# One matrix's load cut differently: w2 in runs of 14 half rows, the remainder in sixteen one-partition loads of prime length on GpSimd's queue

## The chip, the cores and the metric

The kernel runs on one core of a Trainium2 chip, alone. The metric is the device time of one execution in microseconds, as a median of several runs. One profiled execution goes with it: its trace lists every instruction of the compute engines (PE is TensorE, DVE is VectorE, ACT is ScalarE, POOL is GpSimd, SP is SyncE, which here only issues transfers), every packet that the core's 16 DMA engines moved, and every update of a semaphore. "DMA engine" below always means one of those 16; they are not the compute engines.

## The reference

One token passes through two blocks whose results are added: attention over a cache of 65,536 keys in four groups, and a mixer MLP. What matters here:

```
xn = layernorm(x)                                   # x: 1 x 1024
A: q = xn @ wq;  scores, softmax and values over k_cache, v_cache; @ wo
B: h  = gelu(layernorm(xn) @ w1)                    # w1: 1024 x 1024
   g0 = pad(h[:, :, 0:c], ((0,0),(1,0),(0,0)))[:, :S]      # and three more quarters,
   ...                                                     # shifted along the sequence
   hs = concat([g0, g1, g2, g3]) @ w2               # w2: 1024 x 1024
   x1 = xn + hs
   h2 = gelu(layernorm(x1) @ w3) @ w4               # w3: 1024 x 3584, w4: 3584 x 1024
out = x + A + (x1 + h2)
```

The sequence has one token, S = 1, so each of the four quarters is shifted out of sight and `hs` is zero whatever w2 holds. The kernel still loads all of w2 (2 MB, bfloat16) and multiplies it by a column of zeros, `g_col`. All operands are bfloat16; some 170 MB are read, 134 MB of them the two caches.

## The kernel before, in words

Three buffers of 64 KB per partition, `slot0` to `slot2`, take in turn everything that is loaded: wq, w3, w1 with w2, then for eight units K and V (64 KB on each partition, 8 MB a load), then wo, then w4 in five pieces. The list `stream` sets that order and `freed(it)` issues the load that comes three places later, as soon as the instructions that read the slot are recorded. All these loads are issued by SP, in order, and SP waits at each one until its slot is free.

A class `Program` records every operation, and `plan()` derives the waits: an instruction waits for the writers of what it reads and for the readers and writers of what it overwrites. Every transfer has a semaphore of its own that counts to 16. For POOL alone `plan` also makes each operation wait for the one before it on that engine (`last_pool`). The text of `emit` hands the instructions out in the recorded order.

w1 and w2 share a slot (`w12`). Each partition holds 8 rows of w1 (16 KB). w2 is seen as 2,048 half rows of 512 elements (1 KB). A run of `W2_RUN` = 15 of them goes to each of the 128 partitions, in one transfer. The remaining 128 half rows go by `W2_EXTRAS` in two further transfers, on SP too: 20 half rows on each of the partitions 0, 4, 8, 12, 16, and 14 on each of the partitions 1 and 5. Behind the run every partition has room for `W2_DEEP` = 20 half rows. POOL clears that room first (the memset of 128 x 5,120 words), since most partitions get no extra half rows and the multiplication goes over all partitions. The product with w2 is 15 + 20 = 35 matmuls into `psB` (`row_acc` with `g_col`, in `compute_w12`), after which `freed("w12")` issues K of unit 1.

Where the work stands on the queues around the change: POOL makes the identity, the masks and the memsets, the last of them the room behind w2's run, and then copies the queries into `qdiag` when they are there (`place_queries`). SP issues wq at the start, then w3, then w1, w2's run and the two extras. PE waits for w3, w1 and w2 in that order, and DVE starts the first unit's transposes when K of unit 0 has landed.

At the end the fifth piece of w4 (`W4_PIECES`, the last one row of 2 KB per partition) lands, four narrow matmuls use it, ACT and DVE copy the result out, and ACT stores it.

Of the kernel before, what the change touches and what calls it, by code (L numbers as in the profile page):

```python
# [14 lines left out]
P = 128  # L15
# [7 lines left out]
WIDTH = {F32: 4, BF16: 2}  # L23
PITCH = {}
HALF = 512
W2_RUN = 15
W2_EXTRAS = ((0, 5, 20), (1, 2, 14))


def regions(ap):  # L30
# [15 lines left out]
def meet(a, b):  # L46
    return a[0] == b[0] and a[1] < b[2] and b[1] < a[2] and a[3] < b[4] and b[3] < a[4]
# [11 lines left out]
class Program:  # L59
# [74 lines left out]
    def plan(self):  # L134

        known = {e: {} for e in self.engines}
        count = {e: 0 for e in self.engines}
        writers, readers, last_pool = {}, {}, None
        for n, op in enumerate(self.ops):
            e, op.n = op.engine, n  # L140
            need = {}

            def needs(other, raw):
                if other.queue == e and (e in self.IN_ORDER or not raw):
                    return
                if known[e].get(other.queue, 0) < other.at:
                    if other.queue not in need or need[other.queue].at < other.at:
                        need[other.queue] = other

            for r in op.reads:  # L150
                for region_, other in writers.get(r[0], ()):
                    if meet(r, region_):
                        needs(other, True)
            for w in op.writes:
                for region_, other in writers.get(w[0], ()):
                    if meet(w, region_):
                        needs(other, True)
                for region_, other in readers.get(w[0], ()):
                    if meet(w, region_):
                        needs(other, False)  # L160
            if e == "pool" and last_pool is not None:
                needs(last_pool, True)
            picked = sorted(need.values(), key=lambda o: o.n)
            kept = [o for o in picked
                    if not any(o is not x and x.clock.get(o.queue, 0) >= o.at for x in picked)]
            for o in kept:
                o.awaited = True
                for q, at in o.clock.items():
                    known[e][q] = max(known[e].get(q, 0), at)
            op.waits = kept  # L170
            if op.transfer:
                op.queue, op.at = ("dma", n), 1
            else:
                count[e] += 1
                op.queue, op.at = e, count[e]
            if e == "pool":
                last_pool = op
            op.clock = dict(known[e])
            op.clock[op.queue] = op.at
            for w in op.writes:  # L180
                for table in (writers, readers):
                    kept_ = [(r, o) for r, o in table.get(w[0], ())
                             if not (w[1] <= r[1] and r[2] <= w[2] and w[3] <= r[3] and r[4] <= w[4])]
                    table[w[0]] = kept_
                writers[w[0]].append((w, op))
            for r in op.reads:
                readers.setdefault(r[0], []).append((r, op))
# [29 lines left out]
def kernel(  # L217
# [15 lines left out]
    D = A_x.shape[-1]  # L233
# [17 lines left out]
    prog = Program(nc)  # L251
    pe, dve, act, pool = prog, prog.dve, prog.act, prog.pool

    def sb(name, shape, dtype=F32):
        return nc.alloc_sbuf_tensor(name, list(shape), dtype)
# [3 lines left out]

    slots = [sb(f"slot{i}", [P, ROW], BF16) for i in range(3)]  # L260
    PITCH.update({t[:].tensor.name: ROW * 2 for t in slots})
    W2_DEEP = max(m for _, _, m in W2_EXTRAS)
    assert sum(k * m for _, k, m in W2_EXTRAS) == D * D // HALF - P * W2_RUN
    p_sb = sb("p_sb", [P, SUBS * 512], BF16)
    og = sb("og", [P, 512])
    x_row = sb("x_row", [32, D], BF16)
# [32 lines left out]
    tiles = {it: slots[i % 3] for i, it in enumerate(stream)}  # L299

    def load(it):
        t = tiles[it]
        if it == "wq":
            prog.load("sp", t[:], A_wq.rearrange("(p c) n -> p (c n)", c=DC))
        elif it == "w3":
            prog.load("sp", t[:, 0:DC * F], B_w3.rearrange("(p c) f -> p (c f)", c=DC))
        elif it == "w12":
            prog.load("sp", t[:, 0:DC * D], B_w1.rearrange("(p c) n -> p (c n)", c=DC))
            at = DC * D
            halves = B_w2.rearrange("r (h n) -> (r h) n", n=HALF)  # L310
            first = P * W2_RUN
            prog.load("sp", t[:, at:at + W2_RUN * HALF], halves[0:first, :].rearrange("(m c) n -> m (c n)", c=W2_RUN))
            at += W2_RUN * HALF
            for b, k, m in W2_EXTRAS:
                prog.load("sp", t[b:b + 4 * k - 3:4, at:at + m * HALF],
                          halves[first:first + k * m, :].rearrange("(q c) n -> q (c n)", c=m))
                first += k * m
        elif it == "wo":
            prog.load("sp", t[:], A_wo.rearrange("(p j) n -> p (j n)", p=P))
        elif it == "w4":  # L320
            w4_v = B_w4.rearrange("(m c) n -> m c n", c=FC)
            c0 = 0
            for n in W4_PIECES:
                prog.load("sp", t[:, c0 * D:(c0 + n) * D], w4_v[:, c0:c0 + n, :].rearrange("p c n -> p (c n)"))
                c0 += n
        else:
            kind, i = it
            g, b = divmod(i, NB)
            cache = A_k_cache if kind == "K" else A_v_cache
            prog.load("sp", t[:], cache[0, g, b * UKEYS:(b + 1) * UKEYS, :].rearrange("(p ct) d -> p (ct d)", p=P))  # L330

    def freed(it):

        n = stream.index(it) + 3
        if n < len(stream):
            load(stream[n])

    load("wq")
    opening = len(prog.ops)

    dve.memset(x_row[:], 0.0)
    prog.load("act", x_row[0:1, :], A_x[0, 0:1, :])
    load("w3")

    pool.memset(ident_f[:], 0.0)
# [14 lines left out]
    pool.memset(g_col[:], 0.0)  # L360
    w2_end = DC * D + (W2_RUN + W2_DEEP) * HALF
    pool.memset(tiles["w12"][:, w2_end - W2_DEEP * HALF:w2_end].bitcast(F32), 0.0)
    load("w12")

    def row_acc(j, lhsT, rhs, start=False):
        return pe.mm(psB[32 * j:32 * j + 32, :], lhsT.to_broadcast([P, 32]), rhs, start, False, (0, 32 * j), COLS)
# [7 lines left out]
    def layernorm(src, tag):  # L374
        rowsum = sb(f"ln_rowsum_{tag}", [P, 1])
        dve.reduce_sum(out=rowsum[:], in_=src[:], axis=AX.X)
        at = next_pm()
        pe.mm32(at[:, 0:1], ones_f[:], rowsum[:], True, True)
        negmean = sb(f"ln_negmean_{tag}", [P, 1])
        dve.tensor_scalar(out=negmean[:], in0=at[:, 0:1], scalar1=-1.0 / D, scalar2=None, op0=ALU.mult)  # L380
        cen = sb(f"ln_cen_{tag}", [P, DC])
        dve.tensor_scalar(out=cen[:], in0=src[:], scalar1=negmean[:, 0:1], scalar2=None, op0=ALU.add)
        sq = sb(f"ln_sq_{tag}", [P, DC])
        rowsq = sb(f"ln_rowsq_{tag}", [P, 1])
        dve.tensor_tensor_reduce(out=sq[:], in0=cen[:], in1=cen[:], scale=1.0, scalar=0.0,
                                 op0=ALU.mult, op1=ALU.add, accum_out=rowsq[:])
        pe.mm32(at[:, 1:2], ones_f[:], rowsq[:], True, True)
        std = sb(f"ln_std_{tag}", [P, 1])
        act.activation(out=std[:], in_=at[:, 1:2], func=ACTF.Sqrt, bias=eps_t[:, 0:1], scale=1.0 / D)
        rstd = sb(f"ln_rstd_{tag}", [P, 1])  # L390
        dve.reciprocal(out=rstd[:], in_=std[:])
        normed = sb(f"ln_out_{tag}", [P, DC])
        dve.tensor_scalar(out=normed[:], in0=cen[:], scalar1=rstd[:, 0:1], scalar2=None, op0=ALU.mult)
        rep = sb(f"ln_rep_{tag}", [P, DC, 32], BF16)
        dve.tensor_copy(out=rep[:], in_=normed[:].unsqueeze(2).to_broadcast([P, DC, 32]))
        return normed, rep, negmean, rstd

    xn, xn_rep, negmean1, rstd1 = layernorm(xT, "a")
    _, xn2_rep, _, _ = layernorm(xn, "b")
# [53 lines left out]
    def compute_w12():  # L453
# [6 lines left out]
        act.activation(out=h1, in_=sc[0:32, 0:2, :], func=ACTF.Gelu_apprx_tanh)  # L460
        for c in range(W2_RUN + W2_DEEP):
            row_acc(c % 2, g_col[:], wt[:, 2 * DC + c, :], start=(c < 2))
# [86 lines left out]
    for u in range(NU):  # L549
        g, b = divmod(u, NB)  # L550
# [11 lines left out]
    o = tiles["w4"][0:64, FC * D:FC * D + D].bitcast(F32)  # L562
# [76 lines left out]
```

## Time and profile before

| | |
|---|---|
| time, median of 3 runs | 400.24 us (400.12 to 400.31) |
| time of the profiled execution | 400.13 us |
| its span in the trace | 398.8 us |
| busy: PE, DVE, ACT, POOL | 226.0, 210.2, 27.6, 10.6 us |
| mean granted TensorE clock | 0.795 |
| landings on the sixteen DMA engines of the last piece of w4, from the trace's semaphore updates | 394.94, 394.96, 395.29, 395.64, 395.71, 396.29, 396.33, 396.48, 396.49, 396.52, 396.57, 396.65, 396.68, 396.73, 396.74, 396.79 us |

The span leaves 1.33 us of the execution's time outside of it. In the profile's lists a line begins with the source line and engine; `out<-in` are the program's tiles without their buffer number, so `slot` is any of the three slots, and `in_B_w_dram` any of w1 to w4. L92, L99 and L116 are the lines of the recording helpers, so operations are told apart by tiles. A time in square brackets in a timeline is how long the engine sat idle before, and for whom.

### The profile page before, as it was taken

What the parts mean: (1) busy time and instruction counts of PE and PEld (TensorE: products, weight loads), DVE (VectorE), ACT (ScalarE), POOL (GpSimd) and SP (SyncE); (2) the same over time, 40 slices, a digit from 0 to 9 for tenths busy, and PEclk for the clock granted to TensorE, in tenths of its full rate; (3) what the DMA queues carried; (4) which work ended last, traced back from release to release, by engine and by line L of the source; (5) the groups of instructions that cost most, each with busy time, mean ns of one, the idle gap of its engine ahead of it and who ended that gap; (6) DMA issues with size and microseconds to landing.
All of it is one profiled execution on the core that took longest, in us unless ns stands there. A gap on an engine that the chain in (4) does not pass through costs nothing.

```text
span 398.8 us, 2582 instructions
## 1 busy us (share of the span) xinstructions
PE 226.0 (57%) x1379; PEld 45.2 (11%) x890; DVE 210.2 (53%) x156; ACT 27.6 (7%) x35; POOL 10.6 (3%) x30
## 2 busy tenths in 40 slices
PE   0250990592469256923874197529552946393587
PEld 0210000010101020001001000201010102010233
DVE  0520010975096549653963795259439932793411
ACT  1010030002000200020002000200010011002000
POOL 7000000000000000000000000000000000000000
PEclk9996797597859666978796779568967995687669
DMA  8989999999999999999999999999999999999996
GB/s 342 493 375 419 470 427 421 435 460 434 429 421 434 427 435 434 440 440 434 416 434 440 434 421 442 440 427 427 427 449 440 421 434 435 427 427 421 409 438 274
DMA packets 3774, 170.03 MB, mean 426 GB/s; under 512 B 426, under 2 KB 428, under 8 KB 685
## 3 DMA queue, kind: packets, MB, share of 16 engines
q1 hardware_dynamic: 3758, 169.87, 98.8%
q8 instruction: 9, 0.15, 0.1%
q14 instruction: 1, 0.01, 0.0%
q10 hardware_dynamic: 6, 0.00, 0.0%
HBM read 169.87 MB, written 0.00 MB: 426 GB/s over the span
## 4 chain that ended last, share of the span: by engine, by line
DMA 62%; PE 20%; DVE 15%; ACT 2%; issue 0%; SPq 0%
DMA slot<-in_A_k_cache_dram 44%; DMA slot<-in_B_w_dram 18%; PE sc L116 14%; DVE slot L92 11%; PE oacc L116 4%; DVE p_sb L92 2%; DVE mx L92 2%; ACT p_sb L92 2%; PE psB L116 1%; PE pm L132 0%; DVE m L92 0%; DVE rep L92 0%; DVE nball L92 0%; DVE x_halves L92 0%; PE pm L116 0%
## 5 line engine op out<-in xcount | busy, mean ns | idle before, releaser
L116 PE MATMUL sc<-slot,qdiag 128*128 128x512 bf16 x512 | 130.9, 418 | 65.7 <-DVE slot L92 65.6
L92 DVE STREAM_TRANSPOSE slot<-slot 128x4096 f32<-128x4096 f32 x32 | 139.4, 4411 | 52.2 <-DMA slot<-in_A_k_cache_dram 52.2
L116 PE MATMUL oacc<-slot,p_sb 128*32 128x512 bf16 x512 | 44.5, 524 | 37.5 <-DVE p_sb L92 18.8
L92 DVE STREAM_TRANSPOSE p_sb<-p_sb 128x2048 bf16<-128x2048 bf16 (+2 forms) x10 | 20.8, 2085 | 38.7 <-ACT p_sb L92 38.5
L92 DVE TENSOR_REDUCE mx<-sc 128x1 f32<-128x2048 f32 x8 | 18.3, 2292 | 30.6 <-PE sc L116 30.6
L112 PEld LDWEIGHTS <-qdiag 128*128 128x128 bf16 x128 | 13.2, 103 | 181.4 <-issue 181.4
L92 ACT ACTIVATE p_sb<-sc,nball 128x2048 bf16<-128x2048 f32 x8 | 15.7, 1967 | 250.7 <-DVE nball L92 250.7
L112 PEld LDWEIGHTS <-p_sb 128*32 128x32 bf16 x512 | 16.3, 127 | 62.4 <-issue 19.8
L116 PE MATMUL sc<-slot,ln_rep_b 128*32 128x512 bf16 (+1 forms) x80 | 16.2, 828 | 9.1 <-DMA slot<-in_B_w_dram 8.9
L132 PE MATMUL pm<-ident_f,mx 128*1 128x128 f32 x8 | 2.2, 270 | 19.1 <-DVE mx L92 19.1
L92 DVE SCALAR_TENSOR_TENSOR og<-oacc,wb,og 128x512 f32<-128x512 f32 x4 | 3.0, 751 | 18.8 <-PE oacc L116 18.8
L92 POOL COPY qdiag<-qx 32x32 bf16<-32x32 bf16 x16 | 3.2, 203 | 272.5 <-PE sc L116 250.6
L116 PE MATMUL psB<-slot,oT 128*32 128x512 bf16 x64 | 9.2, 457 | 1.2 <-DVE oT L92 1.2
L126 PE MATMUL pm<-ol,selx 128*128 128x129 f32 x8 | 2.6, 415 | 10.6 <-DVE ol L92 10.6
L116 PE MATMUL sc<-slot,ln_rep_a 128*32 128x512 bf16 x64 | 5.7, 532 | 4.4 <-DMA slot<-in_A_wq_dram 4.4
L126 PE MATMUL pm<-ln_rowsum_a,msk 128*128 128x1 f32 x2 | 0.6, 362 | 13.3 <-DVE ln_rowsum_a L92 13.3
L92 DVE TENSOR_TENSOR og<-psB,slot 64x512 f32<-64x512 f32 x1 | 0.7, 683 | 13.1 <-PE psB L116 13.1
L92 DVE STREAM_TRANSPOSE p_sb<-x_row 32x256 bf16<-32x256 bf16 x4 | 2.5, 616 | 7.4 <-DMA x_row<-in_A_x_dram 7.4
L116 PE MATMUL psB<-slot,g_col 128*32 128x512 bf16 x35 | 4.9, 379 | 0.0
L132 PE MATMUL pm<-ident_f,rep 1*128 1x1 f32 x8 | 1.9, 234 | 5.0 <-DVE rep L92 5.0
L92 ACT COPY og<-oacc 128x512 f32<-128x512 f32 x4 | 2.3, 585 | 32.1 <-PE oacc L116 32.1
L116 PE MATMUL psB<-slot,hT 128*32 128x512 bf16 x40 | 4.5, 379 | 0.0
(87 smaller groups left out, 65.5 us busy)
## 6 DMA issues: line engine op xcount, KB each, us to landing
slot<-in_B_w_dram SPq DMA_DIRECT2D x1, 7168.0 KB, 37.3
slot<-in_B_w_dram SPq DMA_DIRECT2D x2, 2048.0 KB, 37.8
slot<-in_B_w_dram SPq DMA_DIRECT2D x1, 3072.0 KB, 33.4
slot<-in_B_w_dram SPq DMA_DIRECT2D x1, 1920.0 KB, 47.2
slot<-in_B_w_dram SPq DMA_DIRECT2D x1, 1280.0 KB, 33.2
slot<-in_B_w_dram SPq DMA_DIRECT2D x1, 512.0 KB, 34.1
slot<-in_B_w_dram SPq DMA_DIRECT2D x1, 256.0 KB, 34.2
slot<-in_A_k_cache_dram SPq DMA_DIRECT2D x8, 42.2
```

The costliest lines, as they stand in the source:

```text
L92: return program.add(Op(engine, lambda: method(*args, **kw), reads, writes, alone=kw.get("accum_out") is not None))
L112: self.add(Op("pe", lambda: pe.ldweights(lhsT, tile_position=pos), [lhsT], []))
L116: return pe.add_instruction(mybir.InstMatmult(name=nc.get_next_instruction_name(), engine=mybir.EngineType.PE, start_tensor_calc=start, st ...
L126: return self.add(Op("pe", lambda: pe.matmul(out, lhsT=lhsT, rhs=rhs, start=start, stop=stop, tile_position=pos, skip_group_check=True), [ ...
L132: return self.add(Op("pe", lambda: pe.transpose(out, in_, identity), [in_, identity], [out]))
```

## The change

- `W2_RUN` goes from 15 to 14: each partition's run is 14 KB.
- The other 256 half rows, 131,072 elements, are cut into sixteen stretches of consecutive elements, each a prime number of elements long (17,401 down to 1,021), and a remainder of 86 elements. Each goes to one partition: 0, 4, ..., 28 for the first eight, 64, 68, ..., 92 for the other eight, and 32 for the remainder.
- The sixteen are issued by POOL, right behind its memset; the remainder by SP, ahead of w1.
- `W2_DEEP` becomes 34, so the memset covers 128 x 8,704 words, and the multiplication with `g_col` has 14 + 34 = 48 matmuls.
- `plan` no longer makes a POOL operation that is a transfer wait for the one before it, nor the next one for the transfer.

```diff
-W2_RUN = 15
-W2_EXTRAS = ((0, 5, 20), (1, 2, 14))
+W2_RUN = 14
+W2_EXTRAS = (17401, 16889, 10223, 11261, 16381, 1021, 1531, 15859, 2557, 3067, 3583, 4093, 4603, 6653, 7673, 8191)
...
-            if e == "pool" and last_pool is not None:
+            if e == "pool" and last_pool is not None and not op.transfer:
                 needs(last_pool, True)
...
-            if e == "pool":
+            if e == "pool" and not op.transfer:
                 last_pool = op
...
-    W2_DEEP = max(m for _, _, m in W2_EXTRAS)
-    assert sum(k * m for _, k, m in W2_EXTRAS) == D * D // HALF - P * W2_RUN
+    W2_DEEP = -(-max(W2_EXTRAS) // HALF)
+    W2_REST = D * D - P * W2_RUN * HALF - sum(W2_EXTRAS)
+    assert 0 < W2_REST <= W2_DEEP * HALF
...
             prog.load("sp", t[:, at:at + W2_RUN * HALF], halves[0:first, :].rearrange("(m c) n -> m (c n)", c=W2_RUN))
-            at += W2_RUN * HALF
-            for b, k, m in W2_EXTRAS:
-                prog.load("sp", t[b:b + 4 * k - 3:4, at:at + m * HALF],
-                          halves[first:first + k * m, :].rearrange("(q c) n -> q (c n)", c=m))
-                first += k * m
...
     pool.memset(tiles["w12"][:, w2_end - W2_DEEP * HALF:w2_end].bitcast(F32), 0.0)
+    w2_flat = B_w2.rearrange("r n -> (r n)")
+    first = P * W2_RUN * HALF
+
+    def w2_piece(engine, p, n):
+        at = w2_end - W2_DEEP * HALF
+        prog.load(engine, tiles["w12"][p:p + 1, at:at + n], w2_flat[first:first + n].rearrange("(o n) -> o n", o=1))
+
+    for e, n in enumerate(W2_EXTRAS):
+        w2_piece("pool", 64 * (e // 8) + 4 * (e % 8), n)
+        first += n
+    w2_piece("sp", 32, W2_REST)
     load("w12")
```

## The prediction, made before the changed kernel ran

> **What bounds the kernel now.** First the page's head: the span, the strip of DMA activity in 40 slices, the queue table and the chain that ended last.
>
> ```profile
> span 398.8 us, 2582 instructions
> ...
> DMA  8989999999999999999999999999999999999996
> ...
> q1 hardware_dynamic: 3758, 169.87, 98.8%
> q8 instruction: 9, 0.15, 0.1%
> ...
> q10 hardware_dynamic: 6, 0.00, 0.0%
> HBM read 169.87 MB, written 0.00 MB: 426 GB/s over the span
> ...
> DMA 62%; PE 20%; DVE 15%; ACT 2%; issue 0%; SPq 0%
> ```
>
> The strip shows the sixteen DMA engines at nine tenths or more nearly everywhere, while PE and DVE are busy 57% and 53%. The chain also names PE and DVE because it passes through instructions that free a slot; but SP issues each load long before the one ahead of it has drained, so the engines have work all the time. The kernel ends when the slowest of the sixteen has moved its share. The end of the chain, in order of time:
>
> ```profile
> 362.56 34.22 DMA slot<-in_B_w_dram
> 396.79 0.04 issue
> 396.83 0.34 PE pm L116 x4
> 397.19 0.43 DVE x_halves L92
> ```
>
> The last piece of w4 lands at 396.79; the 2.0 us behind it are fixed. So the question is which engine lands last, and when.
>
> For that I followed the trace's packet records. A 64 KB packet takes 2.42 us and the next one on its engine starts where it ends, so sixteen chains separate. The sixteen last landings (394.94 to 396.79, mean 396.18) then have reasons. Two engines carry 34 extra half rows and land at 396.29 and 396.33; of the three that carry 20, two land at 395.64 and 395.71, and one, which also moved an 8 KB code packet, near the end. Of the eleven without extras, three land at 394.94, 394.96 and 395.29, and eight at 396.48 or later. Each of these eight has one of PE's code packets in it (the q8 line: nine of 16 KB), which costs its engine about 1.5 us, a gap of 1.0 to 1.1 and a lengthened 64 KB packet. The nine start at 43.3, 104.2, 145.2, 195.9, 242.1, 297.5, 336.4, 377.5 and 396.65; the ninth comes when the last data packet (ends 396.33) is through.
>
> **The change, part by part.** The bytes are the same; only their place changes. A packet of 20 half rows took 0.761 us, so a half row is worth 0.038 us of its engine.
>
> *Shares.* If each prime load is one unsplit transfer on one engine, in turn, engine e gets 14 x 8 half rows and 34, 33, 20, 22, 32, 2, 3, 31, 5, 6, 7, 8, 9, 13, 15, 16, where before it had 15 x 8 and 34, 34, 20, 20, 20 and none. The differences are -8, -9, -8, -6, +4, -6, -5, **+23**, -3, -2, -1, 0, +1, +5, +7, +8, in time -0.34 to +0.87 us. Perfect levelling would bring 396.79 down to the mean, 396.18: 0.61 us is all that there is to gain. The trace doesn't say which engine number each of the eleven chains has. If engine 7 is one of the eight with a code packet (8 chances in 11), it lands at 396.48 to 396.74 plus 0.87: 0.56 to 0.82 later than now, 0.7 in the middle. If it is one of the three early ones, it lands by 396.2, and the end falls to whichever of engines 13, 14, 15 (+0.19 to +0.30) is late: 0.1 to 0.3, say 0.2. Weighted, 0.73 x 0.7 + 0.27 x 0.2 = 0.56; I take **+0.5 us**.
>
> *Are they unsplit?* The nearest row is the one-row load of x, 2 KB: q10's six packets are that load's and the store's, one data packet and one semaphore packet of the load. A row of one partition stays whole on one engine there. That was ACT's queue; for POOL's nothing is shown (a rival below).
>
> *A second queue beside the stream.* The same load shows how a small queue fares:
>
> ```profile
> 2.98 0.53 ACTq L99 DMA_DIRECT2D x_row<-in_A_x_dram  x1
> ...
> 10.35 2.50 DVE L92 STREAM_TRANSPOSE p_sb<-x_row 32x256 bf16<-32x256 bf16 x4 [7.40 <-DMA x_row<-in_A_x_dram]
> ```
>
> Issued at 2.98, it lands at 10.35: in the records its data packet starts at 7.50 and its semaphore packet at 9.99, one 64 KB packet later. So a second queue gets one packet in turn with the stream. It cost the stream 0.07 us for 2 KB, its own bytes and no more. That is the lower bound, and I take it, as the nearest kind (data into a slot's memory). The upper bound is the code packet: 16 KB cost 1.5 us where its bytes at 0.038 are 0.6, a factor of 2.5. At that factor 31 to 34 half rows cost up to 2.0 us more, on engine 7 on top of +0.7: **+2.7 us**. Semaphore packets took 9 ns each; if every load puts one on every engine, 16 are 0.15 us, and I add nothing, since the stream's own 27 show no gap.
>
> *When they land.* Turn by turn, up to 17 packets an engine from about 14 us on: 3 turns in wq's rest, 8 in w3 (its 56 KB packets, to 39.3), 6 of w1's 16 KB packets: all landed by 45 us, before w2's run at 50.
>
> ```profile
> 5.62 4.36 POOL L92 MEMSET slot<- 128x5120 f32 x1
> 31.20 1.00 POOL L92 COPY qdiag<-qx 32x32 bf16<-32x32 bf16 x4 [21.22 <-DVE qx L92]
> ...
> 2.30 9.25 SPq L99 DMA_DIRECT2D slot<-in_B_w_dram  x5
> ...
> SPq L99 <- POOL slot L92: 6.3, 1, 6.3
> ```
>
> *POOL and SP.* The memset grows by 8,704/5,120, to 7.4 us, and ends at 13.0. SP's wait for it, which now stands ahead of w1 at the 86-element load, grows from 6.3 to 9.4; queued behind it are w1 and w2's run, issued by 14.5, while wq and w3 occupy the engines to 39.6: hidden by 25 us. Sixteen issues on POOL cost between SP's 0.33 and ACT's 0.53 us, doubled for safety 17 us: POOL is free at 30, just when the copies into `qdiag` come at 31.2. Those are needed for the first scores, at 74:
>
> ```profile
> 55.71 4.25 PE L116 MATMUL psB<-slot,g_col 128*32 128x512 bf16 x32
> ...
> 59.99 0.33 SPq L99 DMA_DIRECT2D slot<-in_A_k_cache_dram  x1
> 69.75 8.77 DVE L92 STREAM_TRANSPOSE slot<-slot 128x4096 f32<-128x4096 f32 x2 [15.77 <-DMA slot<-in_A_k_cache_dram]
> 74.25 2.29 PE L116 MATMUL sc<-slot,qdiag 128*128 128x512 bf16 x5 [14.29 <-DVE slot L92]
> ```
>
> *PE.* Thirteen more matmuls at 4.25/32 = 0.13 are 1.7 us, and PE waits for 17 semaphores more or less in a row. PE sits idle for 14.29 us behind them; K of unit 1, issued behind them at 59.99, would go out at 61.7 with K and V of unit 0 (to 89 us) still ahead of it. Nothing. Without that cover it would be the 1.7 us.
>
> *Sum.* Span 398.8 + 0.5 = 399.3, execution 400.13 + 0.5 = 400.6; the median stands 0.11 above the profiled execution, so **400.7 us**.
>
> **Rivals.**
> *Foreign packets dear* (slower). POOL's packets cost the stream as code packets do. For: the code packets are the only large foreign ones. Against: the 2 KB load. One or two tenths of the worst case to all of it: +1.0 to +2.7, about 402.2. It decides once the factor is above about 1.3. The Trainium skill (DMA: Bandwidth & Descriptors, Latency and other measured facts) says engines 7 and 15 are usually slower, with software descriptor rings as its guess at the cause; here all sixteen chains show 2.42 us packets without such a queue, so the trace before can't refute it, and the change puts its +23 on engine 7 and +8 on 15.
> *The ninth code packet moves into the end* (slower). PE gets 13 matmuls and 7 wait instructions more, so the ninth fetch comes 20 instructions earlier. PE was 20 records back at about 395.9, so the fetch would start near 396.0, with late engines still moving data to 396.33. If it falls on one of them, their last landing moves by 0.7 to 1.5: with the shares, 401.3. Against: the first eight fell on eight different engines, and most of those left are early.
> *The numbers fit* (faster). Engine 7 early, 13 to 15 not late: -0.1 to -0.6, about 399.9, never below 399.5.
> *They are not spread.* All sixteen on the first engine: 256 half rows against its 34, less 8 of the run, +214 x 0.038 = 8.1 us on an engine that now lands 0.5 early: +7.6, 407.8. For: x's single row is one packet on a single engine. Splitting a prime row element by element is a worse version: 17,401 packets of 9 ns are 157 us, hidden nowhere. The Trainium skill (same page, Why a DMA increments its semaphore by 16 and not by 1) lets a transfer of undividable length use one engine, the next of a rotating cursor on POOL's path, which is the forecast; it also notes direct copies dealt out as partitions over sixteen, which for one partition is this rival. No row here tells.
>
> **How the numbers follow.** Forecast 0.50; dear packets 0.16; ninth packet 0.13; fitting numbers 0.14; not spread 0.07. Forecast's own range is 400.2 to 401.1. The range must leave out the unspread case and the tails: 399.7 to 402.7. Runs of this kernel differ by 0.1 us, and 0.2%, 0.8 us, is about what a measurement tells from no change: 399.4 and 401.0. Faster than that is out of reach of levelling (0.61): 0.05 for what I don't see. Slower: dear packets 0.15, ninth 0.12, unspread 0.07, the forecast's upper tail 0.09: 0.43. Within: 0.52.
>
> **What would show it.** Right: sixteen prime data packets on sixteen engines between 14 and 45 us, 64 KB packets still 2.42 us, the chain's last landing near 397.3, PE idle still about 12 us before the first scores. Wrong: a chain of DMA engine 7 that isn't late, a code packet before the last landing, gaps in the stream beside POOL's packets longer than their bytes, or one engine with all of them and a last landing past 404.

## The result, and the profile after

The changed kernel takes 414.20 us (median of 4 runs, 413.82 to 414.45) where the kernel before takes 400.18 us beside it: a ratio of 1.0349, 95% interval 1.0331 to 1.0367. The forecast was 400.7 us, the range 399.7 to 402.7.

The head of the page after, as it was shown of the kernel before:

```profile
span 412.5 us, 2616 instructions
...
DMA  9998999999999999999999999999999999998950
...
q1 hardware_dynamic: 3746, 169.61, 95.8%
q0 software_dynamic: 512, 0.26, 0.3%
...
HBM read 169.87 MB, written 0.00 MB: 412 GB/s over the span
...
DMA 42%; DVE 26%; PE 21%; another core or an unknown queue 7%; ACT 3%; issue 1%
```

The bytes are the same, but the strip of DMA activity now ends in 8, 9, 5, 0: for the last slices most engines are done. The end in stretches (length, busy time of PE, PEld, DVE, ACT and POOL, granted clock, share of the sixteen DMA engines, GB/s):

```profile
395.00:397.00 2.00, 1.98 (x10) 0.76 (x12) 0.54 (x1) 0.00 (x0) 0.00 (x0) 0.50 0.94 381
397.00:399.00 2.00, 2.00 (x12) 0.78 (x10) 0.00 (x0) 0.00 (x0) 0.00 (x0) 0.50 0.31 122
399.00:404.00 5.00, 5.00 (x46) 2.20 (x42) 0.00 (x0) 0.00 (x0) 0.00 (x0) 0.92 0.06 25
404.00:409.00 5.00, 5.00 (x62) 2.47 (x60) 0.18 (x1) 0.00 (x0) 0.00 (x0) 1.00 0.08 29
```

From 399 to 409 us the DMA share is 0.06 to 0.08 at 25 to 29 GB/s. One engine of sixteen is 0.0625 and 27 GB/s (64 KB in 2.42 us). So **one engine works alone for the last 12 us**. The sixteen landings of the last piece of w4 say the same: fifteen between 396.82 and 398.50, one at 410.45 (before: 394.94 to 396.79). Every load from K of unit 0 on has one landing 12 to 13 us behind the rest. A unit can start only with its last landing, so PE and DVE run late by as much; the chain shows them and the DMA engines by turns. At the very end it shows PE:

```profile
395.02 13.77 PE psB L116 x104
...
410.20 0.63 PE pm L116 x12
```

PE gets to wo and w4 only then (64 and 40 of these matmuls), with a granted clock of 0.50 until 399 us (the last column but two of the stretches above). Its last four matmuls still start 0.05 us behind the landing at 410.45, so the landing sets the end here too, but PE has no more than about 0.2 us to spare.

The packet records don't number the engines, but a packet starts where the one before it on its engine ends, and so the chain of the late engine can be followed. All sixteen prime loads are whole: sixteen data packets of 34,802 down to 2,042 bytes on POOL's queue, q0, and 496 packets of 4 bytes beside them. But all sixteen data packets stand on the *same* engine, each with two packets of the stream between it and the next for most of the way: at 19.61, 23.33, 29.68, 35.23, 41.08 and so on to 62.75 us. The landings of POOL's loads, by size (KB, us from issue to landing):

```profile
slot<-in_B_w_dram POOLq DMA_DIRECT2D x1, 34.0 KB, 10.4
slot<-in_B_w_dram POOLq DMA_DIRECT2D x1, 33.0 KB, 14.1
...
slot<-in_B_w_dram POOLq DMA_DIRECT2D x1, 15.0 KB, 42.2
slot<-in_B_w_dram POOLq DMA_DIRECT2D x1, 16.0 KB, 43.7
```

They land in the order of issue, the smaller later ones last: one line of waiting, not sixteen.

The places that the prediction costed at nothing, from the timelines and SP's waits:

```profile
5.59 7.35 POOL L92 MEMSET slot<- 128x8704 f32 x1
13.24 8.31 POOL L99 DMA_DIRECT2D slot<-in_B_w_dram  x16 [0.30 <-POOL slot L92]
...
SPq L99 <- POOL slot L92: 10.4, 1, 10.4
...
64.63 5.36 PE L116 MATMUL psB<-slot,g_col 128*32 128x512 bf16 x48
70.02 0.33 SPq L99 DMA_DIRECT2D slot<-in_A_k_cache_dram  x1
83.69 8.77 DVE L92 STREAM_TRANSPOSE slot<-slot 128x4096 f32<-128x4096 f32 x2 [21.13 <-DMA slot<-in_A_k_cache_dram]
88.19 4.43 PE L116 MATMUL sc<-slot,qdiag 128*128 128x512 bf16 x10 [18.20 <-DVE slot L92]
```

POOL's memset and issues are done at 21.6, and PE still idles 18.20 us before the first scores. None of them is on the path; DVE waits for K of unit 0, whose last landing is at 83.67.

So 214 half rows too many on one engine explain 8.1 us there, 7.6 at the end, since that engine used to land 0.5 us before the last one. But the end moved by 410.45 - 396.79 = 13.7. The rest, 6 us, had to be found. The fifteen others are late as well: they land 1.7 to 1.9 us later at either end of their field (396.82 against 394.94, 398.50 against 396.79), though each of them carries at least 8 half rows less than before.

### The profile page after: what moved, and what is told of

It is laid out like the page before. It is cut to its first block, busy times and chain, and to the rows that moved or that the text cites. A ratio compares the mean times of both kernels' runs of the same rounds, so it can differ in the third digit from the quotient of the medians.

```text
span 412.5 us, 2616 instructions
## 1 busy us (share of the span) xinstructions
PE 228.4 (55%) x1392; PEld 46.0 (11%) x890; DVE 210.3 (51%) x156; ACT 27.6 (7%) x35; POOL 21.9 (5%) x46
## 4 chain that ended last, share of the span: by engine, by line
DMA 42%; DVE 26%; PE 21%; another core or an unknown queue 7%; ACT 3%; issue 1%
DMA slot<-in_A_k_cache_dram 31%; DVE slot L92 18%; DMA slot<-in_B_w_dram 11%; PE sc L116 11%; PE oacc L116 6%; PE psB L116 3%; DVE p_sb L92 3%; DVE mx L92 3%; ACT p_sb L92 3%; PE pm L132 1%; DVE og L92 1%; PE pm L126 0%; DVE m L92 0%; DVE rep L92 0%
## 5 line engine op out<-in xcount | busy, mean ns | idle before, releaser
L116 PE MATMUL sc<-slot,qdiag 128*128 128x512 bf16 x512 | 129.1, 412 | 68.6 <-DVE slot L92 68.5
L116 PE MATMUL oacc<-slot,p_sb 128*32 128x512 bf16 x512 | 47.4, 551 | 37.5 <-DVE p_sb L92 18.8
L112 PEld LDWEIGHTS <-p_sb 128*32 128x32 bf16 x512 | 17.4, 132 | 64.3 <-issue 23.3
L99 POOL DMA_DIRECT2D slot<-in_B_w_dram x16 | 8.3, 528 | 0.3 <-POOL slot L92 0.3
L92 POOL MEMSET slot<- 128x8704 f32 x1 | 7.4, 7351 | 0.1
L112 PEld LDWEIGHTS <-ln_rep_b 128*32 128x32 bf16 x40 | 1.9, 112 | 30.4 <-issue 30.3
## 6 DMA issues: line engine op xcount, KB each, us to landing
slot<-in_B_w_dram SPq DMA_DIRECT2D x1, 1792.0 KB, 50.9
```

Source lines behind the costliest of these rows:

```text
L92: return program.add(Op(engine, lambda: method(*args, **kw), reads, writes, alone=kw.get("accum_out") is not None))
L99: return self.add(Op(engine, lambda: e.dma_start(out=out, in_=in_), [], [out], transfer=True))
L112: self.add(Op("pe", lambda: pe.ldweights(lhsT, tile_position=pos), [lhsT], []))
L116: return pe.add_instruction(mybir.InstMatmult(name=nc.get_next_instruction_name(), engine=mybir.EngineType.PE, start_tensor_calc=start, st ...
```

## The experiments

Each kernel is compared with runs of the kernel before on the same chip, 400.2 to 400.3 us throughout.

**Who keeps the loads on one engine: the queue or the shape?** The same loads, issued by SP.

```diff
-        w2_piece("pool", 64 * (e // 8) + 4 * (e % 8), n)
+        w2_piece("sp", 64 * (e // 8) + 4 * (e % 8), n)
```

> The sixteen prime loads are issued by SP instead of POOL, all else as in the changed kernel. Theory 'one row, one engine': a load of one partition stays on one DMA engine, the same one each time, whatever the queue; the bytes alone then put 214 half rows x 0.038 = 8.1 us on it, and the last landing comes 7.6 us later than in the kernel before: 407.8 us, up to 414 if the extra 6 us of the changed kernel come from writing into distant partitions and not from having two queues. Rival 'POOL's queue is at fault': issued by SP the loads spread or cost their bytes on sixteen engines: 400 to 401 us. In both, the fifteen other engines lose their 32 small packets each.

414.15 us (ratio 1.0346, 1.0330 to 1.0361), last landings 397.25 to 399.32 and one at 410.88. POOL's queue is not at fault: from SP's queue the loads go to one engine too, at the same cost, and with no second queue to take turns with. The whole of the rest, 6 us, is there as well, which already speaks for the places written to and against turns between two queues.

**Do the prime lengths matter?** On POOL, every length made divisible by 16, within 22 elements of the prime.

```diff
-W2_EXTRAS = (17401, 16889, 10223, 11261, 16381, 1021, 1531, 15859, 2557, 3067, 3583, 4093, 4603, 6653, 7673, 8191)
+W2_EXTRAS = (17392, 16880, 10224, 11264, 16384, 1024, 1536, 15856, 2560, 3072, 3584, 4096, 4608, 6656, 7680, 8192)
```

> The sixteen lengths are multiples of 16 (17,392, 16,880, 10,224 and so on, within 22 elements of the primes), still issued by POOL to the same partitions. Theory 'one row, one engine': the length has no part in it, 414 us as with primes, one landing of each load 12 us behind the others. Rival 'the primes keep the loads whole': loads that divide by 16 are dealt out over sixteen engines, 400 to 401 us, no engine behind.

405.01 us (1.0113, 1.0095 to 1.0132): the rival's mechanism, not its price. The records have sixteen packets for each load (17,392 elements as sixteen of 2,174 bytes), and the landings are all between 398.12 and 401.44. So on POOL's queue the prime length does keep a load whole, and my theory that length plays no part is wrong there. What the change doesn't get is a new engine for each whole load. And dealing out has a price of its own: the landings of the last piece of w4 come 3 us later, mean 399.5 against 396.2. Whether that comes from the 256 small data packets or from where they write, this run doesn't separate.

The same lengths from SP, so this edit and the one before it together:

> The loads of lengths divisible by 16, now issued by SP. Both e2_sixteenths (POOL, dealt out over sixteen engines, 405.0 us) and e1_sp (SP, primes, whole, 414.15 us) are behind this one. 'The length decides' on either queue: sixteen packets to each load, no single late engine, 404 to 406 us. 'SP never deals out one partition' (as the load of x, 1,024 elements in one packet, lets one think): sixteen whole packets on one engine, 413 to 415 us.

414.05 us (1.0344, 1.0327 to 1.0362), one landing at 410.72: from SP the one-partition loads stay whole with either set of lengths. Between these two sets the length makes a difference only on POOL.

**Is it the sum on the engine, or the unequal sizes?** Sixteen POOL loads of 8,191 elements each on the same partitions.

```diff
-W2_EXTRAS = (17401, 16889, 10223, 11261, 16381, 1021, 1531, 15859, 2557, 3067, 3583, 4093, 4603, 6653, 7673, 8191)
+W2_EXTRAS = (8191,) * 16
```

> Sixteen POOL loads of 8,191 elements each, one on each of the same sixteen partitions; the remainder of 16 elements on SP. Theory 'one row, one engine': the sum of the bytes on the one engine is the same, 412 to 415 us. Rival 'the sizes decide' (engine 7's 31 half rows): 400 to 401 us, as every engine would get 128 half rows.

414.62 us (1.0359, 1.0343 to 1.0374). It is 0.4 us slower than the changed kernel, with one landing at 410.85: unequal sizes are not the cause.

**The other 6 us: turns between queues, or crossed writes?** I take it that in the big loads partitions 0, 4, ..., 28 and 64, ..., 92 are filled by sixteen different engines, and partitions 0 to 3 and 32 to 35 by one, the engine that carries the one-partition loads. The trace names no partitions; the packet times below have to bear this out. A write is called *crossed* here when an engine writes into a partition that another one fills in the big loads, and *at home* when it is its own. In the changed kernel one engine writes into all sixteen partitions, and all but one of these writes are crossed. Here the same sixteen loads as in the last run go to partitions 0 to 3 and 32 to 35, two on each, and the 16 elements left over to partition 64.

```diff
-    W2_DEEP = -(-max(W2_EXTRAS) // HALF)
+    W2_DEEP = 32
...
-    def w2_piece(engine, p, n):
-        at = w2_end - W2_DEEP * HALF
+    def w2_piece(engine, p, n, off=0):
+        at = w2_end - W2_DEEP * HALF + off
...
-        w2_piece("pool", 64 * (e // 8) + 4 * (e % 8), n)
+        w2_piece("pool", 32 * (e % 8 // 4) + e % 4, n, 8192 * (e // 8))
...
-    w2_piece("sp", 32, W2_REST)
+    w2_piece("sp", 64, W2_REST)
```

> The same sixteen POOL loads of 8,191 elements, but on eight partitions, 0 to 3 and 32 to 35, two behind each other on each (32 half rows deep, 46 matmuls instead of 48). If the 6 us beyond the bytes in the changed kernel come from one engine writing into partitions that other engines are filling ('crossed writes'), they go and so do most of the 1.8 us that the fifteen other engines lost: 406 to 408.5 us, other engines' last landings 1 us earlier than in the run with sixteen partitions. If they come from taking turns with a second queue ('turns'), nothing changes against that run: 412 to 415 us.

408.02 us (1.0194, 1.0178 to 1.0209). The end of the chain, first with equal loads on sixteen partitions:

```profile
376.40 34.46 DMA slot<-in_B_w_dram
410.85 0.04 issue
410.90 0.34 PE pm L116 x4
```

and then with the same loads on the eight:

```profile
369.87 34.41 DMA slot<-in_B_w_dram
404.28 0.04 issue
404.32 0.34 PE pm L116 x4
```

The last landing comes 6.57 us earlier with the same bytes on the same queue and still on one engine. The fifteen others land at a mean of 395.85 instead of 398.01. The sixteen packets of 16,382 bytes take 0.611 to 0.613 us each; crossed, they took 0.611 to 1.001, and packets of the stream beside them grew too. Added up along the engine of the equal loads, from the first of POOL's packets to the last (14.8 to 62.1 us), the crossed packets are 1.4 us longer than at home, and the stream's own packets between them 4.7 us longer than usual; with home partitions both sums are zero. So the price of the **crossed writes** is shown: 6.6 us on the engine that makes them, most of it in its other packets, and 2.2 us on the others. Nearly all of it (6.5 and 1.9 us) is there by the landing of K of unit 0, before any of the later bursts in the last section. What is left, 404.28 - 396.79 = 7.49 us, is the bytes, priced at 7.6. The 496 small packets are all still there, so they cost nothing that shows.

**Crossed writes by themselves**, on the kernel before: its two extra transfers moved by 64 partitions.

```diff
-W2_EXTRAS = ((0, 5, 20), (1, 2, 14))
+W2_EXTRAS = ((64, 5, 20), (65, 2, 14))
```

> Kernel before with its two extra transfers moved to partitions 64, 68, ..., 80 and 65, 69: the same engines 0 to 4 carry them, but write into partitions that engines 8 to 12 fill. 'Crossed writes': the extra packets take longer than 0.761 and 0.535 us, packets of the stream beside them do too, and engines 8 to 12, some of them late already, land 0.3 to 0.8 later: 400.5 to 401.1 us. If place doesn't matter: 0.761 and 0.535 us again and 400.25 us.

401.50 us (1.0033, 1.0020 to 1.0046), above the range expected. The five packets of 20 half rows took 0.899 to 1.349 us instead of 0.761, the two of 14 took 0.866 and 0.882 instead of 0.535. The surprise is in the stream: sixteen 64 KB packets that start between 48.3 and 50.9 us took 2.75 to 3.81 us (mean 3.46) instead of 2.42, a whole round of all the engines and not only of the five whose partitions are written into. These 1.04 us go into every later landing: the last ones are 396.41 to 398.19 (mean 397.50), against 394.94 to 396.79 (mean 396.18).

**What levelling is worth.** Run of 16, no extras, and so no memset either:

```diff
-W2_RUN = 15
-W2_EXTRAS = ((0, 5, 20), (1, 2, 14))
+W2_RUN = 16
+W2_EXTRAS = ()
...
-    W2_DEEP = max(m for _, _, m in W2_EXTRAS)
+    W2_DEEP = 0
...
-    pool.memset(tiles["w12"][:, w2_end - W2_DEEP * HALF:w2_end].bitcast(F32), 0.0)
```

> Back to SP alone: run of 16 half rows on every partition, no extras, no memset, 32 matmuls with g_col. Measures what the levelling of the kernel before is worth. Engines with a code packet get 8 half rows more than before, 8 x 0.038 = 0.30 us: last landing 397.1 instead of 396.79, so 400.5 to 400.6 us. If the landings are not set by each engine's bytes, 400.25 as before.

400.50 us (1.0006, 0.9998 to 1.0015), last landing 397.16 as worked out. The extras of the kernel before bring about 0.26 us, and the interval of the ratio still contains 1.

**Which engines could take more?** Run of 14 and one load of 32 half rows on engines 0 to 7.

```diff
-W2_RUN = 15
-W2_EXTRAS = ((0, 5, 20), (1, 2, 14))
+W2_RUN = 14
+W2_EXTRAS = ((0, 8, 32),)
```

> Kernel before with a run of 14 and one SP load of 32 half rows on each of the partitions 0, 4, ..., 28 (engines 0 to 7, one each, into the partitions that they serve anyway). If the three early engines of the kernel before are 5, 6 and 7, the engines with code packets land 0.30 earlier than before (396.2 to 396.5) and the last is the one of engines 2 to 4 with its 8 KB code packet, 396.79 + (12 - 8) x 0.038 = 396.9: 400.0 to 400.4 us. If one of 5 to 7 has a 16 KB code packet, it lands at 396.5 to 396.7 + (32 - 8) x 0.038 = 397.4 to 397.7: 400.9 to 401.2 us. No engine is 7 us behind in either.

400.96 us (1.0018, 1.0009 to 1.0027), last landing 397.33. Of the eight engines that carry a 32 KB packet, two also carry a 16 KB code packet, at 104.9 and 146.0 us, and these two and the one with the 8 KB code packet land last (397.24, 397.33 and 396.95; the other thirteen by 396.47). So the second case holds nearly as priced. In the kernel before, none of engines 0 to 4 had a 16 KB code packet. If the code packets go to the same engines in both kernels, which was not tried, it is two of 5, 6 and 7 that have one. All eight packets took 1.213 us, 32 x 0.038: writing at home costs the bytes.

**Does POOL's queue spread anything?** One POOL load of sixteen partitions, 16 half rows on each, with a run of 14:

```diff
...
+    prog.load("pool", tiles["w12"][0:61:4, w2_end - W2_DEEP * HALF:w2_end],
+              w2_flat[first:].rearrange("(q n) -> q n", n=W2_DEEP * HALF))
```

> Run of 14 on SP and one POOL load of 16 half rows on each of the partitions 0, 4, ..., 60. If a POOL load of sixteen partitions is dealt out one partition to an engine, every engine has 128 half rows, with engines 8 to 15 writing 16 half rows into partitions of 0 to 7: 400.6 to 402 us, no single late engine. If POOL's loads all go to one engine whatever their shape: 214 half rows too many again, 407 to 414 us.

401.25 us (1.0025, 1.0015 to 1.0035). POOL's line of its page, beside the 512 packets of the changed kernel:

```profile
q0 software_dynamic: 32, 0.26, 0.2%
```

Sixteen data packets of 16 KB, one on each engine, and sixteen small ones; last landings 395.88 to 397.96, none behind. So this load of several partitions on POOL's queue was dealt out, one partition to an engine. It ends 0.80 us later than the run of 16 (397.96 against 397.16) with the same 128 half rows on every engine: eight of its engines write into partitions that others fill, and fifteen of the stream's packets that start at 15.3 to 16.0 us took 2.70 to 3.04 us.

## Why the prediction was wrong, step by step

*What bounds the kernel* held: in every trace the span ends 2.0 to 2.2 us after the last landing, and a half row is worth 0.038 us on its engine (7.49 us measured for 7.6; 397.16 for 397.1).

*Shares* is the step that failed, in its first condition: "if each prime load is one unsplit transfer on one engine, in turn". Unsplit was right and in turn was wrong: one engine got all sixteen, and its last landing came 13.7 us later instead of 0.5. The table of differences, engine 7's +23 and the 0.5 us worked out from them describe a kernel that never ran. The sentence behind it, on the load of x, could carry neither half. One load can't show where the next one goes. And x has 1,024 elements and came from ACT's queue: a POOL load of just 1,024 elements, in the run with lengths divisible by 16, went in sixteen packets of 128 bytes. So "unsplit" came true because of the prime lengths, and not for the reason that x's row gave. The trace had a hint that I didn't use: x's row lay on an engine that also carried both extra transfers, so transfers with few parts seemed to begin at the same place.

The second thing that failed is a term that was put at nothing: there was none for where a packet writes. The runs put it at 6.6 us on the engine that writes and 2.2 us on the others.

The rule of the Trainium skill that stood for the forecast (DMA: Bandwidth & Descriptors, Why a DMA increments its semaphore by 16 and not by 1), a rotating cursor on POOL's path, is not what these runs show: in three kernels with sixteen whole loads each on POOL (the changed one, the equal loads and the home partitions) all sixteen went to one engine. So they did in two on SP. The Trainium skill's note, in the same section, that some copies are dealt out by partition fits, for one partition and for the sixteen-partition load. The Trainium skill's sentence there that a contiguous length with the divisor 16 can be split fits POOL's loads of such lengths; the same loads from SP stayed whole.

*A second queue beside the stream*: a foreign packet costs its bytes, I said, from 2 KB of x, with a factor of 2.5 from the code packets as the upper bound. The lower bound is right for a write at home (0.611 us for 16,382 bytes) and the factor for a crossed one was 1.2 to 1.8 on the packets themselves where the extras were moved. But most of the price isn't in the packet: it is in the stream's packets beside it (4.7 of 6.1 us in the equal loads). x's row goes to partition 0, at home, so it could not have shown this. And between two of POOL's packets stood mostly two packets of the stream, not one.

*The rival "They are not spread"* is what happened, at a chance of 0.07. Its price, +7.6, is confirmed by the run with home partitions to 0.1 us. It missed the crossed writes, 6.6 us, the other half. Together they make 14.1 for the equal loads' last landing, and the changed kernel's came 13.7 later.

*Foreign packets dear*: not as stated, since SP alone gives the same time. Whether engines 7 and 15 differ from the others, no run here tells. *The ninth code packet* and *the numbers fit* were about tenths of a microsecond on a level field, and there was none. No load was split element by element.

*POOL, SP and PE* held: 8.3 us for sixteen issues (0.52 each, ACT's row), SP waits 10.4 for 9.4, and the idle time of PE before the first scores grew. The landings "by 45 us" came as late as 64.8, because sixteen data packets took turns on one engine instead of one on each.

## What to carry to other kernels

Before putting one-partition loads on different engines, look in the packet records where two of them in a row go: here a whole one-partition load always went to the same engine, and a load was spread only by having several partitions or, on POOL, a length that divides by 16. An engine that writes into partitions which others are filling cost itself 6.6 us here and the others 2.2; the extra bytes cost no more than their size (0.038 us for 1 KB) only where the big loads' own engine put them. With all sixteen engines full, work out first what perfect levelling could bring (0.61 us here), and set it against what a failure puts on one engine (8 us).

No version here beats the kernel before. The engines that would have room (by the two traces, if the code packets go to the same engines in both, one of 5 to 7 and two of 8 to 15, beside those that carry extras now) can't be addressed alone by the loads tried: whole ones went to one engine, and those of several partitions took that one and others with it.

## What was not expected of the hardware

- A one-partition load on POOL's queue is cut into sixteen packets on sixteen engines when its length divides by 16 (17,392 elements: sixteen of 2,174 bytes), and stays whole when it is prime (17,401 elements: one of 34,802 bytes); on SP's queue it stayed whole in both cases (414.05 and 414.15 us).
- Seven crossed packets, 131,072 bytes in all, lengthened one 64 KB packet on all sixteen engines by 1.04 us on average. Why engines whose own partitions weren't touched slow down as well was not tried.
- Around 185 us in the changed kernel some six stream packets took 3.1 to 3.5 us instead of 2.42, and the kernels of the same kind show such bursts at 185, 262 or 340 us; the kernel before and the run with home partitions have none. What sets them off stays open. They are a small part of the price: 0.1 us on the late engine and 0.2 us on the others between the equal loads and the home partitions, and about 0.5 us on the others in the changed kernel.
